# An adding transfer, two rounds for the two largest logits, larger vector instructions and a new order in a gated mix of a long convolution and a routed block

## The chip, the cores and the metric

The kernel runs on one core of a Trainium2 chip. Its engines are TensorE (PE; its weight loads are listed as PEld), VectorE (DVE), ScalarE (ACT), GpSimd (POOL) and SyncE (SP), which here only issues transfers. The metric is the device time of one execution in microseconds; the figure used is the median of several.

## The reference

Two results of the same input `x` (2048 tokens, 512 channels, bfloat16) are mixed token by token by a sigmoid gate.

```python
x = A_u
g = sigmoid((x * gate_w).sum(-1, keepdims=True))
# a: a state-space convolution: per channel a kernel K of 2048 lags, applied by FFT
dt = exp(log_dt)[:, None];  A = A_re + 1j * A_im;  dB = dt * (B_re + 1j * B_im)
P = exp((dt * A)[:, :, None] * l)              # 512 x 128 modes x 2048 lags
K = einsum("dn,dnl,dn->dl", C, P, dB).real
y = irfft(rfft(x, 4096) * rfft(K, 4096))[:2048] + x * Dskip
# b: two tokens are routed through a gated block
r = x @ w_r;  idx = argsort(-r)[:2]
b = x;  b[idx] += ((silu(x[idx] @ w_gate) * (x[idx] @ w_up)) @ w_down) * sigmoid(r[idx])
out = g * y + (1 - g) * b
```

## The kernel before

The kernel is one list of 558 operations, made by the function's helpers in the order of the source. Two hand-kept lists decide how it runs: `PLAN` gives every operation its place in one global order and, by its second number, which of its possible engines runs it; `BANKS` gives the PSUM banks. Each engine, and SP and POOL as issuers of transfers, runs its operations in PLAN's order, strictly one after the other; `emit_plan` adds the semaphore waits that the data need. So an operation that waits holds everything behind it on its engine.

The convolution is done in two blocks of 1024 tokens with a transform of 1024 points that leaves even and odd parts apart, and the modes are summed through a factorisation of each lag into a coarse and a fine part. The channels are worked in two halves (hf or c, 0 and 1). The stages, in the names of the program:

- *Set-up*: the parameters are loaded (`nat0` to `nat5`) and turned on PE by the identity matrix `CI` (`turned`, L572), which is loaded as `cia` (L525). `al` is the first DVE operation, the decay rates; ACT then runs exponentials of it (`ep`, `eq`, `ek`), and the phases follow on DVE (`bs`, `bn`, `hi`, `lo`, `psi` and others, part polar). `kw` holds the modes' weights, and its polar form goes over `ln`, `ab`, `lr`, `rec` on ACT and `sm`, `qx`, `pz`, `as` on DVE.
- *transform(m)* for block m: the loads of u (`ul`, L549) and of the transform's constants (`fl`, L551), each in two parities, are multiplied on PE (L870), evicted with factor 1 or -2 (`fwe`, `fwo`), and summed: `vb` are two transfers from POOL that add one buffer to another in SBUF (L881, L883), `v1` and `v0` two DVE sums of 2048 elements, `w1` and `w0` four DVE sums of 1024 elements per block (L886 to L888).
- *moduli, weigh*: products of the exponentials on DVE.
- *coarse(hf), fine(hf)*: PE adds up phases in PSUM (L681, L686), ACT takes sines (L437); coarse multiplies them into the table TP on DVE (`ns`, `pi`, `pr`), fine into TQ by the weighting `qm` (L727), five instructions of 2048 elements per half.
- *rows*: the transposed input `xt` is loaded by a transposing transfer (L565), PE makes the gate's and the router's logits (`log`, L744), DVE copies them. The two largest logits and their token numbers are found in four rounds of `gmax` (L766): a reduction of 16 to 1 per partition, a matmul with the identity that brings all 128 partitions' values to each partition, and a reduction of 128 to 1 from PSUM; twice for the value, twice for the index, with `cand`, `sel` and `mask` between them. Small sigmoids run on POOL. The two rows of u are gathered (`gu`), turned (`gat`), copied by ACT (`xs`), and go through the weights `wg`, `wu`, `wd`. `uc` (L839) copies u to a table in HBM, into which `sc` writes the two changed rows; `ue` and `u2` load from it. `z1` is ACT's scaling of the result by `rs`, which comes from POOL (`rsf`).
- *lags(c)*: PE sums the modes (`kmm`, L923), the result is evicted (`kae`), re-ordered by selecting matmuls (`sel`, L937) and evicted (`kce`, `kcx`); *spectrum(c)* (L962, L967) needs the constants `kn` in four pieces (L1143) and is evicted as `khe`, `khf`.
- *products(c,j)* on DVE (L1007, and sums such as `acc`, `yr`, `yi`, `pq`, `b0`, `b2`, `b13`), partly summed on PE (`ac`, L1030 to L1034); *inverse(c,j)* on PE (L1109 to L1114), evicted with the gate as scale (`ive`, L1125, L1129) and sent out. `residual` makes the diagonals `rd` that add the gated input on PE.

Most DVE operations are recorded at the line of their helper: `TT` is L408, so groups under L408 mix many stages.

Of the kernel before, what the change touches and what calls it, by code (L numbers as in the profile page):

```python
# [9 lines left out]
BF = mybir.dt.bfloat16  # L10
# [169 lines left out]
PLAN = [(0, 0), (4, 0), (5, 0), (6, 0), (7, 0), (8, 0), (9, 0), (10, 0), (11, 0), (12, 0), (13, 0), (14, 0), (3, 0), (27, 0), (1, 1), (48, 0),  # L180
# [47 lines left out]
NG = 4  # L228
# [91 lines left out]
def bass_gated_mix__ssm_conv_s4__moe_arch_mod__prompt_kernel(nc, A_u, A_A_re, A_A_im, A_B_re, A_B_im, A_C_re, A_C_im, A_log_dt, A_Dskip,  # L320
# [15 lines left out]
    for m_ in range(2):  # L336
        for q_ in range(2):
            for r_ in range(4):
                cf[:, 128 + (m_ * 2 + q_) * 4 + r_] = 4096.0 - token(m_, q_, r_)
    cf[0, 144] = 1.0  # L340
    cf[1, 145] = 1.0
    cf[0, 147] = -1.0
    cf[1, 148] = -1.0
    cf[:, 149] = 1.0e-36
    cf[:, 150] = alt
    cf[:, 151] = -alt
    cf_c = nc.inline_tensor(cf, "c_f32").ap()
    near, far = lag_mats()
# [892 lines left out]
```

## Time and profile before

| | |
|---|---|
| median of 3 runs | 147.81 us (147.77 to 147.84) |
| the profiled execution's own time | 148.18 us |
| its span, first to last instruction | 146.4 us |
| granted TensorE clock | 0.987 |
| PE busy | 128.3 us (88%), 1302 instructions |
| DVE busy | 135.5 us (93%), 174 instructions |
| ACT busy | 114.5 us (78%), 162 instructions |
| POOL busy | 18.1 us (12%), 30 instructions |
| moved by DMA | 26.46 MB, mean 181 GB/s |
| chain that ended last | DVE 44%, PE 33%, ACT 18%, issue 3% |

Busy times count instructions from start to end. Matmuls and vector instructions overlap their neighbours a little, so busy shares of a row can pass what is really used; the distance between two starts is the surer measure. The chain that ended last goes back from the last instruction, at each step to what released it or to the instruction before it on its engine. A group in the list by line and form gives busy time, mean nanoseconds of one instruction, and the idle time ahead of it. A transfer's row gives the KB of one and the time from issue to landing.

### The profile page before, as it was taken

What the parts mean: (1) busy time and instruction counts of PE and PEld (TensorE: products, weight loads), DVE (VectorE), ACT (ScalarE), POOL (GpSimd) and SP (SyncE); (2) the same over time, 40 slices, a digit from 0 to 9 for tenths busy, and PEclk for the clock granted to TensorE, in tenths of its full rate; (3) what the DMA queues carried; (4) which work ended last, traced back from release to release, by engine and by line L of the source; (5) the groups of instructions that cost most, each with busy time, mean ns of one, the idle gap of its engine ahead of it and who ended that gap; (6) DMA issues with size and microseconds to landing.
All of it is one profiled execution on the core that took longest, in us unless ns stands there. A gap on an engine that the chain in (4) does not pass through costs nothing.

```text
span 146.4 us, 3151 instructions
## 1 busy us (share of the span) xinstructions
PE 128.3 (88%) x1302; PEld 89.0 (61%) x1309; DVE 135.5 (93%) x174; ACT 114.5 (78%) x162; POOL 18.1 (12%) x30
## 2 busy tenths in 40 slices
PE   7956719999999979999979998888999898999992
PEld 3842306654434656566735886865888676778881
DVE  0699999989999999999999999999999999999962
ACT  3699999799999989699957878998499734517731
POOL 2000000180304804145310000000000000000000
PEclk9999999689999999999999999999999999999999
DMA  4779999899970809989646693735380050001345
GB/s 135 248 242 236 278 271 258 317 356 321 297 169 0 143 6 318 468 311 285 129 145 177 148 425 158 203 72 222 21 288 0 0 146 4 0 0 40 107 138 150
DMA packets 23741, 26.46 MB, mean 181 GB/s; under 512 B 9224, under 2 KB 20112, under 8 KB 23568
## 3 DMA queue, kind: packets, MB, share of 16 engines
q1 hardware_dynamic: 21134, 23.46, 52.4%
q0 software_dynamic: 1088, 2.10, 7.9%
q10 hardware_dynamic: 1506, 0.72, 1.7%
q8 instruction: 10, 0.16, 0.5%
q14 instruction: 3, 0.02, 0.0%
HBM read 19.85 MB, written 4.20 MB: 164 GB/s over the span
## 4 chain that ended last, share of the span: by engine, by line
DVE 44%; PE 33%; ACT 18%; issue 3%; POOL 0%; DVEq 0%; POOLq 0%
DVE RB L408 36%; ACT RB L437 11%; PE psm L1114 10%; ACT RB L428 6%; PE psm L962 5%; PE psm L1030 4%; DVE RB L434 3%; PE psm L1109 2%; PE psm L937 2%; PE psm L1034 2%; PE psm L1032 2%; DVE RB L706 2%; PE psm L535 2%; PE psm L681 1%; ACT L1186 1%
## 5 line engine op out<-in xcount | busy, mean ns | idle before, releaser
L408 DVE TENSOR_TENSOR RB<-RB 128x2048 bf16<-128x2048 bf16 (+8 forms) x120 | 113.0, 987 | 1.4 <-ACT RB L437 0.2
L428 ACT ACTIVATE RB<-psm 128x1024 bf16<-128x1024 f32 (+7 forms) x44 | 38.1, 898 | 15.4 <-PE psm L1034 9.2
L437 ACT ACTIVATE RB<-psm 128x1024 bf16<-128x1024 int16 (+1 forms) x37 | 36.5, 1033 | 6.4 <-PE psm L686 2.8
L1114 PE MATMUL psm<-RB 128*128 128x256 bf16 x160 | 22.3, 273 | 0.0
L681 PE MATMUL psm<-RB 128*128 128x256 f16 (+1 forms) x112 | 21.1, 336 | 0.2 <-ACT RB L428 0.2
L870 PE MATMUL psm<-RB 128*128 128x512 bf16 x61 | 15.0, 383 | 5.8 <-ACT RB L428 3.8
L437 ACT ACTIVATE RB<-RB 128x512 bf16<-128x512 f32 (+5 forms) x32 | 16.7, 591 | 1.3 <-DVE RB L408 1.2
L1114 PEld LDWEIGHTS psm<-RB 128*128 128x128 bf16 x160 | 15.7, 98 | 1.8
L686 PE MATMUL psm<-RB 128*128 128x512 f16 x44 | 13.5, 393 | 2.8 <-ACT RB L437 2.8
L962 PE MATMUL psm<-RB 128*128 128x256 bf16 x128 | 15.1, 273 | 0.8 <-ACT RB L428 0.8
L681 PEld LDWEIGHTS psm<-RB 128*128 128x128 f16 x112 | 10.8, 101 | 8.0 <-issue 0.5
L870 PEld LDWEIGHTS psm<-RB 128*128 128x128 bf16 x64 | 6.0, 100 | 14.5 <-ACT RB L428 4.7
L962 PEld LDWEIGHTS psm<-RB 128*128 128x128 bf16 x128 | 12.3, 98 | 3.4 <-ACT RB L428 1.6
L1125 ACT ACTIVATE RB<-psm,RB 128x256 bf16<-128x256 f32 x25 | 10.2, 472 | 5.2 <-PE psm L1114 4.2
L923 PE MATMUL psm<-RB 128*128 128x80 bf16 x256 | 10.4, 198 | 0.5 <-ACT RB L428 0.4
L923 PEld LDWEIGHTS psm<-RB 128*128 128x128 bf16 x256 | 9.7, 96 | 1.7 <-ACT RB L428 1.0
L1109 PE MATMUL psm<-RB 128*128 128x256 bf16 x32 | 8.7, 273 | 0.6 <-DVE RB L408 0.4
L428 ACT ACTIVATE RB<-psm,RB 128x1024 bf16<-128x1024 f32 (+1 forms) x9 | 9.2, 1062 | 0.0
L686 PEld LDWEIGHTS psm<-RB 128*128 128x128 f16 x44 | 3.5, 100 | 6.7 <-ACT RB L437 5.9
L1030 PE MATMUL psm<-RB 128*128 128x512 bf16 x21 | 6.5, 380 | 0.8 <-ACT RB L428 0.6
L883 POOL DMA_DIRECT2D RB<-RB x2 | 2.6, 1321 | 32.6 <-ACT RB L428 32.6
L434 DVE CAST RB<-psm 128x1024 bf16<-128x1024 f32 (+3 forms) x6 | 6.4, 1062 | 0.0
(71 smaller groups left out, 119.7 us busy)
## 6 DMA issues: line engine op xcount, KB each, us to landing
RB<-in_A_u_dram SPq DMA_DIRECT2D x8, 256.0 KB, 4.4
RB<-RB POOLq DMA_DIRECT2D x4, 512.0 KB, 9.8
RB<-c_near SPq DMA_DIRECT2D x4, 512.0 KB, 6.5
RB<-c_inv SPq DMA_DIRECT2D x1, 2048.0 KB, 10.4
RB<-u_routed SPq DMA_DIRECT2D x2, 1024.0 KB, 5.4
RB<-in_B_w_gate_dram SPq DMA_DIRECT2D x1, 1792.0 KB, 9.4
RB<-in_B_w_up_dram SPq DMA_DIRECT2D x1, 1792.0 KB, 16.8
RB<-in_B_w_down_dram SPq DMA_DIRECT2D x1, 1792.0 KB, 7.5
```

The source lines that it names most:

```text
L408: return P.add(name, [(eng, c_dve(n, mode) if eng == DVE else 1.0, lambda h: h.tensor_tensor(out=o(), in0=a_(), in1=b_(), op=op))], rd, wr ...
L428: return lambda h: h.activation(out=o(), in_=a_(), func=ACTF.Copy, scale=scale() if callable(scale) else scale)
L434: return P.add(name, [(ACT, c_act(n), f_act(o, a_)), (DVE, c_dve(n, 1), lambda h: h.tensor_copy(o(), a_()))], rd, wr, **kw)
L437: return P.add(name, [(ACT, cost or c_act(n), lambda h: h.activation(out=o(), in_=a_(), func=func, scale=scale))], rd, wr, table=table, **kw)
L681: r = h.matmul(P32(t, 0, 0, 128, 256 * l0, (1, 256 * nl)), DGM(0, 128, (DD.index(d) + 2) * 128, (1, 128)), src(0, 128, col + hf * CW, (0, ...
L686: r = h.matmul(P32(t, b, 0, 128, 0, (1, 512)), DGM(0, 128, 0, (1, 128)), DGM(0, 128, 128 + c_, (0, 512)), start=False, stop=False, skip_gr ...
L870: x = h.matmul(P32(t, b, 0, 128, 0, (1, 512)), FM(0, 128, 2048 * par + 1024 * pl + 512 * i + 256 * q + 128 * b, (1, 128)), U(0, 128, ((m * ...
L923: x = h.matmul(P32(t, q // 6, 0, 128, (q % 6) * 80, (1, 80)), TPv(0, 128, ri * 16384 + c * 8192 + r * 128, (1, 128)), TQv(0, 128, c * 1024 ...
L962: x = h.matmul(P32(t, kt // 2, 0, 128, (kt % 2) * 256, (1, 256)), KN(0, 128, 2048 * KNP[2 * pl + hc] + 512 * g + 128 * kt, (1, 128)), KC[c ...
L1030: r = h.matmul(P32(t, kt, 0, 128, 0, (1, 512)), CI(0, 128, 0, (1, 128)), f(k, 0, 512), start=(k == 0 and hc == 1), stop=False, skip_group_ ...
L1109: h.matmul(o, RD(0, 128, (tb + 8) % 16 * 128, (1, 128)), UE[q](0, 128, r * 256, (1, 256)) if early else U2(0, 128, tb * D + c * CW, (1, 25 ...
L1114: x = h.matmul(o, G(0, 128, (pl * 4 + kt) * 1024 + (r * 2 + q) * 128, (1, 128)), PQ(0, 128, r * 1024 + kt * 256 + pl * 256 if quarter else ...
```

## The change

The new list has 546 operations. By edit:

- In block 1 the sum `v0` leaves DVE; a third adding transfer from POOL (`vd`) does it, after `v1`.
- `w1` and `w0` become one DVE sum of 2048 elements each per block. So that both planes have the same sign, one plane of the odd part is built from the other parity's summand first (the order of r in `transform`).
- `qm`, the weighting, takes groups 0 and 1, then 2 and 3, then 4: two instructions of 4096 elements and one of 2048 per half.
- The two largest logits: `top` replaces `gmax`, with DVE's eight-largest instruction (`max`). Two rounds instead of four; each brings the largest and second of every partition to all partitions by two matmuls, and takes the eight largest of 256 in PSUM. The two token numbers are found in one round, by coding the rank into the candidates. Two small POOL operations (`ix1`, `ix2`) are added ahead of `idx`.
- The identity `cia` is built on POOL, by a memset and two affine selects, instead of being loaded.
- The constants of the transform and `kn` lie in HBM piece by piece, so that each load is one contiguous block.
- `hh` moves from POOL to DVE.
- `PLAN` and `BANKS` are new. DVE has 163 operations instead of 174, ACT 143 instead of 147 (its transfers included), POOL 31 instead of 26, PE 161 instead of 163 groups of matmuls. Among others, `xt` is issued ahead of the transform's second-parity loads, `uc` ahead of `wg` and `gu`, `c_inv` (the inverse's constants) ahead of the last two pieces of `kn`, and some evictions change sides between ACT and DVE.

```diff
-        DMA("cia", lambda h: [h.dma_start(CI(0, 128, 0, (1, 256)), dr(id_c, 0, (640, 128), (1, 256)))], [], [bCIA], 64, rate=200.0, also=(ACT,))
+        P.add("one", [(POOL, 0.25, lambda h: h.memset(ONE(0, 128, 0, (1, 128)), 1.0))], [], [bONE])
+        P.add("id0", [(POOL, 0.25, lambda h: h.memset(CI(0, 128, 0, (1, 256)), 0.0))], [], [bCIA])
+        P.add("id1", [(POOL, 0.35, lambda h: h.affine_select(out=CI(0, 128, 0, (1, 128)), in_=CI(0, 128, 0, (1, 128)), compare_op=ALU.not_equal, fill=1.0, base=0, pattern=[[-1, 128]], channel_multiplier=1))], [bCIA], [bCIA])
+        P.add("id2", [(POOL, 0.35, lambda h: h.affine_select(out=CI(0, 128, 128, (1, 128)), in_=CI(0, 128, 128, (1, 128)), compare_op=ALU.not_equal, fill=-1.0, base=0, pattern=[[-1, 128]], channel_multiplier=1))], [bCIA], [bCIA])
...
-                TT("qm", q, q, lambda G_=G_: MQ(0, 128, hf * 5120 + G_ * 1024, (0, 2), (1, 1024)), ALU.mult, bQS[G_][hf] + [bMW[hf] if G_ < 2 else bMF[G_][hf]], [bQF[G_][hf]], 2048)
+                for gs in ((0, 1), (2, 3), (4,)):
+                    if gs[-1] != G_:
+                        continue
+                    q = lambda gs=gs: TQv(0, 128, hf * 10240 + gs[0] * 1024, (5120, 2), (1, 1024 * len(gs)))
+                    TT("qm", q, q, lambda gs=gs: MQ(0, 128, hf * 5120 + gs[0] * 1024, (0, 2), (1, 1024 * len(gs))), ALU.mult, ..., 2048 * len(gs))
...
+        def top(src, bsrc, tag):
+            P.add("gm", [(DVE, 0.17, lambda h: h.max(out=RT["pm"](0, 128, 0, (1, 8)), in_=src(0, 128, 0, (1, 16))))], [bsrc], [bRT["pm"]])
+            t = P.pst(1, "gm")
+            def gt(h, t=t):
+                for k in range(2):
+                    r = h.matmul(P32(t, 0, 0, 128, 128 * k, (1, 128)), RT["pm"](0, 128, k, (0, 128)), CF(0, 128, 0, (1, 128)), start=True, stop=True)
+                return r
+            MM("gt", gt, [bRT["pm"], bCF], [t], 1.0)
+            P.add("gm2", [(DVE, 0.43, lambda h, t=t: h.max(out=RT[tag](0, 128, 0, (1, 8)), in_=P32(t, 0, 0, 128, 0, (1, 256))))], [t], [bRT[tag]])
...
+        top(rb2, brb2, "m1")
+        STT("cand", row(cand, 0, 16), row(rb2, 0, 16), one1("m1"), idx, ALU.is_ge, ALU.add, [brb2, bRT["m1"], bCF], [bcand], 16)
+        STT("cand", row(cand, 0, 16), row(rb2, 0, 16), two1("m1"), row(cand, 0, 16), ALU.is_ge, ALU.mult, [brb2, bRT["m1"], bcand], [bcand], 16)
+        top(cand, bcand, "v1")
...
-            TT("v0", vs(0, 0, 0, 1024), vs(0, 0, 0, 1024), vs(1, 1, 0, 1024), ALU.add, bVs[m][0][0] + bVs[m][1][1], bVs[m][0][0], 2048)
-            for hc in (1, 0):
-                for pl in range(2):
-                    TT("w%d" % hc, vs(1, hc, pl, 512), vs(1, 0, pl, 512), xs(1 - pl, 512), ALU.add if pl == hc else ALU.subtract, [bVs[m][1][0][pl], bXO[m][1 - pl]], [bVs[m][1][hc][pl]], 1024)
+            if m in [1]:
+                DMA("vd", lambda h, lo=lo: [h.dma_start(lo(0, 0), lo(1, 1), accum_op=ALU.add)], bVs[m][0][0] + bVs[m][1][1], bVs[m][0][0], 512, eng=POOL, issue=1.3, lat=3.8, rate=155.0)
+            else:
+                TT("v0", vs(0, 0, 0, 1024), vs(0, 0, 0, 1024), vs(1, 1, 0, 1024), ALU.add, ..., 2048)
+            ws = lambda hc: (lambda: V(0, 128, vo[m][1] + hc * 1024, (vo[m][3] - vo[m][1], 2), (512, 2), (1, 512)))
+            xw = lambda: XO[m](0, 128, 1024 * m + 512, (-1024 if m else 1024, 2), (-512, 2), (1, 512))
+            TT("w1", ws(1), ws(0), xw, ALU.subtract, bVs[m][1][0] + bXO[m], bVs[m][1][1], 2048)
...
+                TT("w0", ws(0), ws(0), xw, ALU.add, bVs[m][1][0] + bXO[m], bVs[m][1][0], 2048)
...
-            DMA("kn", lambda h, i=i: [h.dma_start(KN(0, 128, 2048 * KNP[i], (1, 2048)), dr(kn_c, 2048 * i, (8192, 128), (1, 2048)))], [], [bKN[i]], 512, rate=330.0)
+            DMA("kn", lambda h, i=i: [h.dma_start(KN(0, 128, 2048 * KNP[i], (1, 2048)), dr(kn_c, 2048 * 128 * i, (2048, 128), (1, 2048)))], [], [bKN[i]], 512, rate=370.0)
```

More of the change, by code (lines that the diff above doesn't have):

```diff
@@ L407, in TT @@
         def TT(name, o, a_, b_, op, rd, wr, n, mode=2, eng=DVE, **kw):
-            return P.add(name, [(eng, c_dve(n, mode) if eng == DVE else 1.0, lambda h: h.tensor_tensor(out=o(), in0=a_(), in1=b_(), op=op))], rd, wr, **kw)
+            return P.add(name, [(eng, c_dve(n, mode) if eng == DVE else 1.8, lambda h: h.tensor_tensor(out=o(), in0=a_(), in1=b_(), op=op))], rd, wr, **kw)
         def TS(name, o, a_, s1, op0, rd, wr, n, mode=1, s2=None, op1=None, eng=DVE, **kw):
@@ L414, in TS @@
                 f = lambda h: h.tensor_scalar(out=o(), in0=a_(), scalar1=s1() if callable(s1) else s1, scalar2=s2() if callable(s2) else s2, op0=op0, op1=op1)
-            return P.add(name, [(eng, c_dve(n, mode) if eng == DVE else 1.0, f)], rd, wr, **kw)
+            return P.add(name, [(eng, c_dve(n, mode) if eng == DVE else 1.8, f)], rd, wr, **kw)
         def TSA(name, o, a_, s1, s2, rd, wr, n, mode):
@@ L421, in PC @@
         def PC(name, o, a_, rd, wr):
-            return P.add(name, [(POOL, 0.9, lambda h: h.tensor_copy(o(), a_()))], rd, wr)
+            return P.add(name, [(POOL, 1.8, lambda h: h.tensor_copy(o(), a_()))], rd, wr)
         def STT(name, o, a_, sc, b_, op0, op1, rd, wr, n, **kw):
@@ L470, in bass_gated_mix__ssm_conv_s4__moe_arch_mod__prompt_kernel @@
         RT = {}; bRT = {}
-        for k in ("pm", "m1", "v1", "m2", "v2", "rs0", "rsr", "rs", "ix0", "ix1"):
-            RT[k], bRT[k] = small("rt_" + k, 4, F32)
+        for k, n_ in (("pm", 8), ("m1", 8), ("v1", 8), ("rs0", 1), ("rsr", 1), ("rs", 1), ("ix0", 1), ("ix1", 1)):
+            RT[k], bRT[k] = small("rt_" + k, 4 * n_, F32)
         IDX, bIDX = small("idx", 4, I32)
@@ L531, in bass_gated_mix__ssm_conv_s4__moe_arch_mod__prompt_kernel @@
         row = lambda v, c=0, n=D: (lambda: v(0, 128, c, (1, n)))
-        P.add("one", [(POOL, 0.3, lambda h: h.memset(ONE(0, 128, 0, (1, 128)), 1.0))], [], [bONE])
         twm = P.pst(1, "hm")
@@ L768, in gmax @@
             t = P.pst(1, "gm")
-            MM("gt", lambda h, t=t: h.matmul(P32(t, 0, 0, 128, 0, (1, 128)), RT["pm"](0, 128, 0, (0, 128)), CF(0, 128, 0, (1, 128)), start=True, stop=True), [bRT["pm"], bCF], [t], 0.5)
-            P.add("gm2", [(DVE, 0.29, lambda h, t=t: h.tensor_reduce(out=RT[tag](0, 128, 0, (1, 1)), in_=P32(t, 0, 0, 128, 0, (1, 128)), axis=AX.X, op=ALU.max))], [t], [bRT[tag]])
+            def gt(h, t=t):
+                for k in range(2):
+                    r = h.matmul(P32(t, 0, 0, 128, 128 * k, (1, 128)), RT["pm"](0, 128, k, (0, 128)), CF(0, 128, 0, (1, 128)), start=True, stop=True)
+                return r
@@ L788, in token_of @@
+        TS("ix1", one1("ix1"), two1("v1"), 1.0, ALU.is_ge, [bRT["v1"], bCF], [bRT["ix1"]], 1, s2=lambda: CF(0, 128, 153, (1, 1)), op1=ALU.mult, eng=POOL)
+        TT("ix2", one1("ix0"), one1("ix0"), one1("ix1"), ALU.add, [bRT["ix0"], bRT["ix1"]], [bRT["ix0"]], 1, 1, eng=POOL)
+        STT("idx", lambda: IDX(0, 2, 0, (1, 1)), lambda: CF(0, 2, 148, (1, 1)), lambda: RT["v1"](0, 2, 1, (1, 1)), lambda: RT["ix0"](0, 2, 0, (1, 1)), ALU.mult, ALU.add, [bRT["v1"], bRT["ix0"], bCF], [bIDX], 1)
         def token_of(h, k):
@@ L863, in transform @@
                 tiles = [P.pst(2, "fw") for pl in range(2)]
-                for i, r in enumerate((par + 2, par)):
+                for i in range(2):
                     for pl in range(2):
+                        r = par + 2 * (i == 0) if not (par and not pl) else par + 2 * i
                         def fw(h, t=tiles[pl], i=i, r=r, pl=pl, par=par):
```

55 lines of the change are left out of this document (27 added, 28 removed), and 68 rows, old and new, of the table PLAN.

## The prediction

> **What bounds the kernel now.** I read the page first (busy shares), then the busy time by stretch, then the chain that ended last, then the groups by form, and last the queues.
>
> ```profile
> span 146.4 us, 3151 instructions
> ...
> PE 128.3 (88%) x1302; PEld 89.0 (61%) x1309; DVE 135.5 (93%) x174; ACT 114.5 (78%) x162; POOL 18.1 (12%) x30
> ```
>
> ```profile
> 4.90:30.00 25.10, 17.51 (x144) 10.70 (x145) 24.42 (x40) 23.40 (x38) 1.30 (x3) 0.93 1.00 271
> 30.00:60.00 30.00, 28.21 (x249) 15.68 (x250) 29.14 (x44) 28.30 (x34) 10.55 (x15) 1.00 0.74 204
> 60.00:90.00 30.00, 27.92 (x362) 19.30 (x360) 29.90 (x35) 24.51 (x30) 5.39 (x9) 1.00 0.78 255
> 90.00:140.00 50.00, 47.26 (x507) 37.94 (x509) 49.38 (x54) 35.10 (x57) 0.00 (x0) 1.00 0.29 82
> ```
>
> The columns after the length are PE, PEld, DVE and ACT busy. From 4.9 to 140 us DVE is busy 132.8 of 135.1 us: it is the bound for the whole body, and a DVE instruction taken out there is time taken out, as long as something else does not become late. ACT is nearly full until 60 us (51.7 of 55.1) and free after that; PE is nearly full from 90 us on. From 140 us on there is only a tail of a few matmuls, four evictions and the output.
>
> ```profile
> 43.83 1.24 DVE RB L408
> 45.09 4.51 DVE RB L408 x4
> ...
> 96.91 0.27 PE psm L1109
> ```
>
> In the chain, four independent products start 1.13 us apart (4.51 over 4), but one whose successor needs its result keeps the next waiting 1.26 (43.83 to 45.09): a gap of about 0.12. From 96.91 on the chain runs over PE, though DVE is just as full there: both matter.
>
> **The change part by part.** Durations are of this profiled execution, whose own time is 148.18 us for a span of 146.4; the median of the runs is 147.81, 0.37 lower, so I take the sum off 147.81.
>
> ```profile
> L408 DVE TENSOR_TENSOR RB<-RB 128x2048 bf16<-128x2048 bf16 x60 | 71.3, 1218 | 0.7
> L408 DVE TENSOR_TENSOR RB<-RB 128x1024 bf16<-128x1024 bf16 x31 | 20.5, 686 | 0.2
> L408 DVE TENSOR_TENSOR RB<-RB 128x4096 bf16<-128x4096 bf16 x4 | 9.1, 2281 | 0.0
> L770 DVE TENSOR_REDUCE RB<-psm 128x1 f32<-128x128 f32 x4 | 1.1, 284 | 0.4 <-PE psm L769 0.4
> L767 DVE TENSOR_REDUCE RB<-RB 128x1 f32<-128x16 f32 x4 | 0.7, 168 | 0.1
> L425 DVE SCALAR_TENSOR_TENSOR RB<-RB 128x16 f32<-128x16 f32 x2 | 0.4, 210 | 0.0
> L414 DVE TENSOR_SCALAR RB<-RB 128x16 f32<-128x16 f32 x1 | 0.2, 234 | 0.0
> L408 DVE TENSOR_TENSOR RB<-RB 128x16 f32<-128x16 f32 x1 | 0.2, 175 | 0.0
> L759 DVE RECIPROCAL RB<-RB 128x16 f32<-128x16 bf16 x1 | 0.2, 246 | 0.0
> L759 DVE RECIPROCAL RB<-RB 128x1 f32<-128x1 bf16 x1 | 0.2, 157 | 0.0
> ```
>
> An instruction starts some 0.083 before the one ahead of it ends (1.218 against the spacing of 1.13), so I count 1.135, 0.603 and 2.20 us for 2048, 1024 and 4096 elements.
>
> *Adding transfer*: one sum of 2048 less: -1.13.
>
> *Larger sums*: eight of 1024 become four of 2048: 8 x 0.603 - 4 x 1.135 = -0.28. *Larger weighting*: ten of 2048 become four of 4096 and two of 2048: 11.35 - 11.07 = -0.28.
>
> *Largest two*: twelve instructions go, 4 x 0.284 + 4 x 0.168 + 2 x 0.210 + 0.234 + 0.175 = 2.64 busy; the 0.4 wait for the broadcast matmul and the gaps of this dependent chain about cancel the overlap, so 2.64 of the line. Six come: two reductions of 16 (0.085 of spacing), two of 256 from PSUM, two 0.21 with gaps of 0.12. Eight-largest has no row. Lower end: as a reduction, 0.284 + 128 x 0.00104 = 0.42, spacing 0.33 (0.00104 us an element is 0.284 less 0.15 over 128). Upper end: the reciprocal's rate, (0.246 - 0.157) / 15 = 0.006 an element, 1.67 us for 256. I take the lower, since the reduction is the same walk over the same PSUM row: 0.17 + 0.66 + 0.5 = 1.33, so -1.3; the other end is 2.7 dearer.
>
> ```profile
> L434 DVE CAST RB<-psm 128x1024 bf16<-128x1024 f32 x2 | 2.4, 1212 | 0.0
> L434 DVE CAST RB<-psm 128x960 bf16<-128x960 f32 x2 | 2.3, 1151 | 0.0
> L1159 DVE TENSOR_TENSOR RB<-RB 128x1024 bf16<-128x1024 bf16 x1 | 1.2, 1206 | 0.0
> ```
>
> *Sides in the new order* (PLAN's second number picks the engine): off DVE go one spectrum eviction (1.13) and the residual's diagonals (1.12); onto it come one lag eviction of 960 (1.07), and one of 320, a negation, a 32x256 copy and three tiny ones (hh among them), by their sizes an estimated 1.2: nothing on balance (+0.05). On ACT the diagonals are eight instructions, about 2.8 us, laid beside the selecting matmuls, where ACT is free after 60 us: nothing, or up to 1 us if the spectrum's evictions come late by it.
>
> *Gaps*: counted in the two lists, outside the largest-two chain, some 29 neighbours need the result just ahead, 18 in the new one: 11 x 0.12 = -1.3.
>
> ```profile
> 4.91 0.69 DVE L408 TENSOR_TENSOR RB<-RB,psm 128x512 f32<-128x512 bf16 x1 [4.91 <-PE psm L572]
> ...
> 1.31 0.38 ACTq L525 DMA_DIRECT2D RB<-c_id  x1
> 3.87 0.60 ACT L437 ACTIVATE RB<-psm 128x512 bf16<-128x512 f32 x1 [1.86 <-PE psm L539]
> ...
> RB<-c_id ACTq DMA_DIRECT2D x1, 64.0 KB, 2.3
> ...
> 0.72 0.20 POOL L532 MEMSET RB<- 128x128 bf16 x1 [0.29 <-POOLq L1226]
> ```
>
> *Identity on POOL*: the identity lands at 1.31 + 2.3 = 3.6 now, the turns (L572) start at 3.8, DVE at 4.91, while the other operand is ready at 4.47. A memset of 256 and two affine selects after 0.92 cost 0.2 each at the memset's rate, 1.2 at the dearer small POOL row below: ready at 1.5 to 4.0. The first turn alone then frees DVE at 4.55: -0.35, between -0.35 and +0.2.
>
> *Constants by piece* have no row for the contiguous form; their loads are two or more us ahead of use, so nothing either way; cover gone, PE waits for 512 KB, 1.9 us at the 271 GB/s of the first stretch.
>
> ```profile
> 8.71 11.56 SPq L446 DMA_TRANSPOSE RB<-in_A_u_dram  x1
> ...
> RB<-in_A_u_dram SPq DMA_TRANSPOSE x1, 13.7
> ...
> DMA packets 7932, 2.07 MB, mean 259 GB/s; under 512 B 7911, under 2 KB 7925, under 8 KB 7932
> ...
> L744 PE MATMUL psm<-RB x64: 167/172/173, 24.2 to 26.2; 128*128 128x2 bf16 x64
> ```
>
> *The new order's head*: the logits' copy moves from DVE 27.9 to about 20.4 (sum of the DVE rows ahead of it). It needs the transposed load plus 2.3 us of matmuls. Now issued at 8.7 and landed at 22.4, its 256 B packets move from 14 to 22 us (the third row is of that window), behind two loads of 512 KB. The new list puts it ahead of those, at about 6.4; then its packets can run from about 9.5, and 7.5 us of them end at 17 to 18: no wait. If it keeps its 13.7, it lands at 20.1, the copy at 22.5: a wait of 2.0. The two loads behind it (transform 0's second half) land at 21 to 25 against a need at 24 to 26.
>
> *Waits that stay or come*: the old list carries about 1.3 us of them on DVE beside the 0.4 above. In the new one I find, adding rows on both sides: qx waits for the reciprocal on ACT (17.0 us of ACT rows after 5.25) 0.8; the second product waits for c_near's last piece, which now lies behind the 2 MB of c_inv on SP, 0.9; the first lag eviction and the first product 0.5; spectrum 1's evictions are due within 0.6 us of the product that reads them. With something unseen, 2.8, between 1 and 6.
>
> ```profile
> L883 POOL DMA_DIRECT2D RB<-RB x2: 1266/1321/1376, 28.7 to 64.3; - x2
> ...
> DMA to landing us min/median/max: 5.1/9.8/14.5
> ...
> L412 POOL TENSOR_SCALAR RB<-RB 128x16 bf16<-128x16 bf16 x1 | 1.2, 1172 | 0.1
> ...
> L414 POOL TENSOR_SCALAR RB<-RB 128x16 bf16<-128x16 bf16 x1 | 0.2, 208 | 0.0
> ```
>
> *Queues*: the new transfer waits for v1 (DVE, about 67.5) and holds POOL 1.3 us; even 14.5 us later its sum is there at 82, and its first reader is a product at about 104. Behind it on POOL stand sgo twice, omg and rsf, 0.2 to 1.2 each; ACT's z1 at about 75.5 needs rsf, ready at 72 to 74.7: covered by 1 to 3 us. If not, z1 holds ACT and the spectrum's evictions. Small POOL rows of one shape differ sixfold here (0.208, 1.172). The Trainium skill, SBUF — State Buffer, section Who interferes with whom, says that a VectorE instruction with two SBUF inputs blocks a GpSimd one that reads SBUF until it ends; by that rule the 4096-element weighting beside omg and rsf makes them later by about 1 us, which the cover still holds; the spread of the rows agrees with it. ix1 and ix2 come before idx with 6 us of DVE work between: covered.
>
> *Tail*: same last matmuls and outputs, 0, within 0.6.
>
> **Sum**: -1.13 - 0.28 - 0.28 - 1.3 + 0.05 - 1.3 - 0.35 = -4.6; old waits -1.3, new ones +2.8: -3.1. 147.8 - 3.1 = 144.7.
>
> **The rivals.**
>
> *PE sets the end.* Its last stretch starts when spectrum 1 is done, which follows fine 1's last weighting; by the same sum DVE reaches that 2.6 us earlier (the gaps saved behind it, some 0.5, left out). One more inverse piece (0.55) comes after spectrum 1, and PE's late waits may add 0.5: -1.5, 146.3. Against it: lag evictions start on a free ACT in the new list.
>
> *Eight-largest is dear*: -3.1 + 2.7: 147.4.
>
> *The transposed load keeps its length*: -3.1 + 2.0 = 146.7.
>
> *The larger instructions do not run at two elements a cycle* (the change not doing what it says): the four sums with reversed blocks at 1 ns an element, 4 x 1.05 = +4.2: 148.9. The b13 sums already have reversed blocks among the 686 ns group: unlikely.
>
> *Slower: the two chosen rows arrive late.*
>
> ```profile
> RB<-in_A_u_dram SPq DMA_DIRECT2D x1, 256.0 KB, 10.0
> ...
> 40.41 0.20 DVE L425 SCALAR_TENSOR_TENSOR RB<-RB 2x1 int32<-2x1 f32 x1
> ...
> 47.55 0.17 ACT L428 ACTIVATE RB<-psm 128x8 bf16<-128x8 f32 x1
> ...
> RB<-in_B_w_gate_dram SPq DMA_DIRECT2D x1, 1792.0 KB, 9.4
> ...
> u_routed<-in_A_u_dram SPq DMA_DIRECT2D x1, 12.6
> ```
>
> A 256 KB load issued behind the gate weights took 10.0 us: SP's loads go in turn. The new list puts the 2 MB copy of u and the gate weights ahead of the two gathered rows, whose turned form ACT copies (xs, now at 47.55) at about 40.9, in line with the sines. Now xs starts 7.1 after idx (40.41), with ACT busy ahead of it; the new list has idx at 34, so xs at 41.1 or sooner, no wait worth naming if the queue is empty by 38. From 17.5 on it carries 1.9 MB of smaller loads, the copy's 2 MB and 1.8 MB of gate weights: at the 271 GB/s of the first stretch above, 21 us, so 38.5. At the rows' full times (24 + 12.6 + 9.4) it empties at 46: ACT waits 6, DVE, which runs a us behind the sines, 4.5: +1.4, 149.2. It decides from a landing after about 44. The Trainium skill, DMA: Bandwidth & Descriptors, section Queues, rings and completion order, says that each engine takes a ring's descriptors in order; by that the gathered rows wait for all of both, which the 10.0 agrees with.
>
> **How the numbers follow.** Forecast, 142.8 to 146.0: 0.58. PE's end and the long transposed load, 146.0 to 147.4: 0.20; dear eight-largest, about 147.4, and no change: 0.09, of which 0.07 within 0.2%; slower (late rows, slow sums, unseen): 0.10; better than 142.8: 0.03. 0.2%, 0.3 us, is what these runs can tell from no change. Faster 0.83, same 0.07, slower 0.10. Range for 8 in 10: 142.8 (new waits about 1 us: -5.0) to 147.8 (new waits 6, or no change).
>
> **What would show it.** Right: DVE busy about 131 (one eviction of 512 leaves its tail too), first DVE at 4.5, spacing 2.2 in the weighting, transposed load landed by 18, last b13 sum ended near 137 instead of 140. Wrong: a wait ahead of xs on ACT, of the logits' copy or of the second product on DVE over 2 us, eight-largest over 1 us, or DVE ending early and PE still running on.

## The result, and the profile after

The changed kernel takes 147.21 us in the median of 20 runs, the kernel before 148.26 beside it on the same chip: ratio 0.991 (95% interval 0.989 to 0.994), some 1.3 us faster. The forecast was 3.1 us faster, 144.7. The profiled execution takes 147.33 us against 148.18: 0.85 less. Its page:

```profile
span 145.5 us, 3147 instructions
...
PE 128.9 (89%) x1303; PEld 88.9 (61%) x1309; DVE 131.8 (91%) x163; ACT 115.4 (79%) x167; POOL 27.3 (19%) x35
```

DVE is busy 3.7 us less, about as forecast (131.8, "about 131"), but the span is only 0.9 us shorter: DVE now stands still more. Groups by form:

```profile
L411 DVE TENSOR_TENSOR RB<-RB 128x2048 bf16<-128x2048 bf16 x55 | 65.7, 1219 | 0.5
...
L411 DVE TENSOR_TENSOR RB<-RB 128x4096 bf16<-128x4096 bf16 x8 | 18.2, 2287 | 1.0 <-ACT RB L431 0.9
...
L898 POOL DMA_DIRECT2D RB<-RB x1 | 1.2, 1200 | 6.4 <-DVE RB L411 6.4
...
L782 DVE MAX8 RB<-psm 128x8 f32<-128x256 f32 x2 | 0.9, 428 | 1.0 <-PE psm L779 1.0
...
L775 DVE MAX8 RB<-RB 128x8 f32<-128x16 f32 x2 | 0.4, 178 | 0.1
```

Eight-largest cost the lower end of its bounds (0.18 and 0.43 us), and the larger instructions keep the pace of the others: 2.29 us for 4096 elements, 1.22 to 1.23 for each of the four sums with reversed blocks, as for every other sum of 2048. What DVE waited for (total us, times, longest):

```profile
DVE RB L411 <- PE psm L577: 4.9, 1, 4.9
DVE RB L1150 <- PE psm L1135: 2.1, 3, 1.6
DVE RB L782 <- PE psm L779: 1.0, 1, 1.0
DVE RB L411 <- ACT RB L431: 0.9, 2, 0.6
DVE RB L428 <- POOL RB L411: 0.8, 1, 0.8
DVE RB L411 <- DMA RB<-in_A_C_im_dram: 0.5, 1, 0.5
```

The first row is the start, the second the tail. The other four are the new waits: before the first eight-largest of 256 (its broadcast matmul), before the first two products (evictions of spectrum 0), before `idx` (POOL), and before the second `bc` (the load of C's imaginary part). A shorter one, 0.23, stands before the logits' copy. Counted as the distance of two starts less an undisturbed spacing, which takes in the restart, all these are 3.9 us up to the last b13 sum, against 1.55 before. "Waits" below are counted so.

The tail is 6.27 us after the end of the last b13 sum (140.12 before, 139.27 after), in both kernels and within 0.02 in every run below: that end is the time. The profiled execution of idx_later below is one of its slow ones (its ratio is not), so it is read up to 45 us only.

### The profile page after: what moved, and what is told of

It is laid out like the page before. It is cut to its first block, busy times and chain, and to the rows that moved or that the text cites. A ratio compares the mean times of both kernels' runs of the same rounds, so it can differ in the third digit from the quotient of the medians.

```text
span 145.5 us, 3147 instructions
## 1 busy us (share of the span) xinstructions
PE 128.9 (89%) x1303; PEld 88.9 (61%) x1309; DVE 131.8 (91%) x163; ACT 115.4 (79%) x167; POOL 27.3 (19%) x35
## 4 chain that ended last, share of the span: by engine, by line
DVE 61%; PE 15%; ACT 8%; DMA 6%; POOL 5%; issue 2%; SPq 1%; ACTq 0%
DVE RB L411 54%; ACT RB L440 6%; POOL RB L417 5%; DMA RB<-c_near 3%; DMA RB<-in_A_C_im_dram 3%; ACT RB L431 3%; PE psm L686 2%; PE psm L1135 2%; PE psm L882 2%; DVE RB L437 2%; PE psm L691 2%; PE psm L752 1%; PE psm L983 1%; PE psm L944 1%; SPq L533 1%
## 5 line engine op out<-in xcount | busy, mean ns | idle before, releaser
L411 DVE TENSOR_TENSOR RB<-RB 128x2048 bf16<-128x2048 bf16 (+9 forms) x111 | 110.4, 1045 | 2.0 <-ACT RB L431 0.9
L431 ACT ACTIVATE RB<-psm 128x1024 bf16<-128x1024 f32 (+7 forms) x42 | 37.5, 918 | 12.6 <-PE psm L1055 8.8
L440 ACT ACTIVATE RB<-psm 128x1024 bf16<-128x1024 int16 (+1 forms) x37 | 36.2, 1015 | 6.3 <-PE psm L691 2.8
L882 PE MATMUL psm<-RB 128*128 128x512 bf16 x60 | 16.8, 408 | 3.4 <-DVE RB L434 2.8
L1146 ACT ACTIVATE RB<-psm,RB 128x256 bf16<-128x256 f32 x27 | 10.7, 491 | 4.9 <-PE psm L1135 4.3
L417 POOL TENSOR_SCALAR RB<-RB 128x1 f32<-128x1 f32 (+3 forms) x6 | 11.8, 1973 | 4.0 <-DVE RB L782 3.8
L411 POOL TENSOR_TENSOR RB<-RB 128x1 f32<-128x1 f32 (+3 forms) x5 | 1.5, 304 | 38.9 <-DVE RB L782 22.4
L1051 PE MATMUL psm<-RB 128*128 128x512 bf16 x22 | 6.7, 380 | 0.2
```

Of the source, the lines that this page charges most:

```text
L411: return P.add(name, [(eng, c_dve(n, mode) if eng == DVE else 1.8, lambda h: h.tensor_tensor(out=o(), in0=a_(), in1=b_(), op=op))], rd, wr ...
L417: f = lambda h: h.tensor_scalar(out=o(), in0=a_(), scalar1=s1() if callable(s1) else s1, scalar2=s2() if callable(s2) else s2, op0=op0, op ...
L431: return lambda h: h.activation(out=o(), in_=a_(), func=ACTF.Copy, scale=scale() if callable(scale) else scale)
L440: return P.add(name, [(ACT, cost or c_act(n), lambda h: h.activation(out=o(), in_=a_(), func=func, scale=scale))], rd, wr, table=table, **kw)
L882: x = h.matmul(P32(t, b, 0, 128, 0, (1, 512)), FM(0, 128, 2048 * par + 1024 * pl + 512 * (r < 2) + 256 * q + 128 * b, (1, 128)), U(0, 128, ...
L1146: x = h.activation(out=OT[k](0, 128, ocol(q, r), (1, 256)), in_=P32(t, 0, 0, 128, q * 256, (1, 256)), func=ACTF.Copy, scale=SGF["gc"](0, 1 ...
```

## The experiments

All are the changed kernel with the edit shown, and each ratio is to the kernel before, timed beside it. `PLAN`'s entries are named instead of numbered. The runs were made in groups, and the ratio of one program moves between them: the changed kernel itself has 0.989 in the group of idx_later, index_on_dve and broadcast_first (after_again) and 0.994 in that of best_eviction (after_last; 0.989 to 0.992 was expected). The other groups have no run of it. For each run the trace gives the start of `idx`, the end of the last b13 sum, and the waits up to it:

| run | ratio (95%) | waits | idx | b13 end | between |
|---|---|---|---|---|---|
| changed kernel | 0.991 (0.989-0.994) | 3.9 | 36.20 | 139.27 | 103.1 |
| after_again | 0.989 (0.983-0.994) | 4.0 | 36.37 | 139.34 | 103.0 |
| after_last | 0.994 (0.991-0.997) | 2.9 | 35.47 | 138.52 | 103.1 |
| idx_later | 0.998 (0.993-1.004) | | 37.58 | | |
| index_on_dve | 0.984 (0.979-0.990) | 2.9 | 36.02 | 139.04 | 103.0 |
| broadcast_first | 0.982 (0.976-0.988) | 2.4 | 34.69 | 137.88 | 103.2 |
| broadcast_again | 0.984 (0.980-0.988) | 1.7 | 34.70 | 137.46 | 102.8 |
| both_head | 0.989 (0.985-0.993) | 3.0 | 35.82 | 139.20 | 103.4 |
| head_order | 0.992 (0.989-0.996) | 2.3 | 35.90 | 138.66 | 102.8 |
| narrow | 0.991 (0.988-0.995) | 1.9 | 35.31 | 138.27 | 103.0 |
| sum_back | 0.998 (0.994-1.002) | 3.4 | 35.73 | 139.93 | 104.2 |
| sums_early | 0.988 (0.984-0.993) | 4.3 | 36.40 | 139.53 | 103.1 |
| all_order | 0.989 (0.985-0.993) | 2.9 | 35.67 | 139.07 | 103.4 |
| inverse_later | 1.011 (1.006-1.016) | 5.1 | 35.07 | 140.54 | 105.5 |
| gaps_fewer | 0.997 (0.994-1.000) | 5.0 | 35.84 | 139.77 | 103.9 |
| gaps_out | 1.019 (1.013-1.025) | 9.2 | 36.16 | 143.70 | 107.5 |
| waits_out | 1.003 (0.999-1.008) | 4.5 | 35.37 | 140.50 | 105.1 |
| best_eviction | 0.987 (0.981-0.993) | 2.8 | 34.44 | 138.25 | 103.8 |

best_order (1.014, 1.008-1.020) stands with inverse_later below. Two things to read: from `idx` on, the changed kernel and the versions near it all need 102.8 to 103.4 us; and the same program reaches `idx` at 35.5 to 36.4.

**What idx waits for.** after_again is the base of its group.

> The changed kernel itself, as the base of this group. Both theories: 0.991 of the kernel before, DVE's waits for other engines again near 3.9 us up to the last b13 sum (0.60 before bc, 1.05 before the eight-largest of 256, 0.90 before idx, 0.65 and 0.45 before the first two products).

idx_later puts `idx` behind the next product:

```diff
-... cm, idx, wg, fw, pi, ns ...
+... cm, wg, fw, pi, idx, ns ...
```

> Only idx, the VectorE step that waits for GpSimd's ix0, ix1 and ix2, stands one product (pi, 1.14 us) later in VectorE's order. Theory A (GpSimd's ix0 takes its 6.3 us by itself): GpSimd is done at 36.2 whatever VectorE does, idx starts at 36.5 without a wait, and the kernel is 0.9 us faster than the changed one (0.985 of before). Theory B (ix0 can't get at SBUF while VectorE's instructions follow one another without a gap, and ended at 35.6 only because VectorE had run out of work at 35.4): with one more product ahead ix0 lasts about 1.1 us longer, the wait before idx is 0.6 to 0.9 again, and the time is that of the changed kernel within 0.3 us.

POOL and DVE in the timeline (start, us; in brackets the idle time before it), the changed kernel first:

```profile
29.29 6.61 POOL L417 TENSOR_SCALAR RB<-RB 128x1 f32<-128x1 f32 x2 [3.76 <-DVE RB L782]
```

```profile
33.16 2.22 DVE L411 TENSOR_TENSOR RB<-RB 128x2048 bf16<-128x2048 bf16 x2
36.20 0.21 DVE L428 SCALAR_TENSOR_TENSOR RB<-RB 2x1 int32<-2x1 f32 x1 [0.82 <-POOL RB L411]
```

and idx_later:

```profile
29.53 7.74 POOL L417 TENSOR_SCALAR RB<-RB 128x1 f32<-128x1 f32 x2 [3.77 <-DVE RB L782]
```

```profile
33.40 3.35 DVE L411 TENSOR_TENSOR RB<-RB 128x2048 bf16<-128x2048 bf16 x3
37.58 0.20 DVE L428 SCALAR_TENSOR_TENSOR RB<-RB 2x1 int32<-2x1 f32 x1 [0.82 <-POOL RB L411]
```

With one more product ahead, POOL's two one-element instructions took 1.13 us longer, and the wait came out the same (0.90 in both). So theory A is out: what DVE runs beside it holds `ix0` (6.31 of the 6.61 us here), which ended some 0.2 us after DVE had run dry. That it always takes a break of DVE, as theory B has it, is not so: see broadcast_first below. The Trainium skill, SBUF — State Buffer, section Who interferes with whom, says that a VectorE instruction with two SBUF inputs contends with a GpSimd one that reads SBUF, and that of two that contend the later waits until the other has finished. The trace agrees in kind, but the hold here was longer than one instruction: eight of DVE's ran meanwhile. Theory B's time did not come out either: the ratio is 0.7% over the changed kernel's 20 runs, 1.0% over after_again's, where it forecast 0.2% at most. Why stays open; the index comes 1.2 to 1.4 us later, and so does what is gathered by it.

index_on_dve removes `eng=POOL` from `ix0`, `ix1` and `ix2`:

> ix0, ix1 and ix2 run on VectorE instead of GpSimd, at the same places of the order. Both theories of ix0: the 0.90 us wait before idx goes, three instructions of one element come, some 0.1 to 0.2 us each with their gaps: 0.3 to 0.6 us faster than the changed kernel. msb on GpSimd, which now comes first there, lasts until VectorE leaves a gap (theory B: over 2 us; theory A: under 0.5 us). Rival for the whole: ScalarE's sines are the bound up to 60 us, and what VectorE saves here it waits for later: no difference at the end.

The wait before `idx` is gone. The ratio, 0.984 beside after_again's 0.989, points the way that was forecast, but their intervals overlap, and in the one profile the last b13 sum ends only 0.3 us earlier than in after_again's. `msb` now took 0.35 us on POOL, at 24.7, beside DVE's dependent chain of candidates, where the same instruction had taken 3.0 at 36.2. A wait of 0.98 before the second eight-largest had come instead.

**What is paid in the head.**

```diff
-... log, pa (coarse 0), ..., qx, gt, ...
+... log, ..., qx, gt, pa (coarse 0), ...
```

> On TensorE the first broadcast of the two largest (fp32 matmuls) stands ahead of the first phases of coarse 0 instead of behind them. Theory (a wait on VectorE is paid in full, since VectorE is full behind it): the 1.05 us wait before the eight-largest of 256 goes and the end comes 0.8 to 1.05 us earlier than in the changed kernel (0.984 to 0.986 of before). Rival (ScalarE's sines are the bound here, since the first one of coarse 0 starts as much later): a wait of VectorE for a sine takes its place between 27 and 50 us, and the time is that of the changed kernel within 0.3 us.

> broadcast_first once more, as the base of this group: the span about 144.1, VectorE's waits 2.4 us up to the last b13 sum, 0.982 of before. Rival (its 1.2 us against the changed kernel were the chip of that group): 0.99 of before.

`idx` starts 1.5 us earlier than in the first profile of the changed kernel, and the end comes 1.4 to 1.8 us earlier (0.6 to 1.1 against its fastest profile, after_last). The waits of broadcast_first:

```profile
DVE RB L411 <- ACT RB L431: 1.1, 2, 0.6
DVE RB L411 <- DMA RB<-in_A_C_im_dram: 0.8, 1, 0.8
DVE RB L434 <- PE psm L752: 0.2, 1, 0.2
```

Neither broadcast nor `idx` is among them, though `ix0` is still on POOL. POOL, then DVE:

```profile
28.68 3.66 POOL L417 TENSOR_SCALAR RB<-RB 128x1 f32<-128x1 f32 x2 [3.91 <-DVE RB L782]
```

```profile
32.55 2.22 DVE L411 TENSOR_TENSOR RB<-RB 128x2048 bf16<-128x2048 bf16 x2
34.69 0.20 DVE L428 SCALAR_TENSOR_TENSOR RB<-RB 2x1 int32<-2x1 f32 x1
```

DVE ran the same instructions from the second eight-largest to `idx`, again without a break, and `ix0` took 1.73 us and not 6.31. It did so in all four profiles with this order on TensorE and the index on POOL (sums_early and best_eviction below are the others); in the nine with the old order it took 6.31 (7.44 in idx_later). In the four, DVE had waited 0.13 to 1.26 us just before that eight-largest; in the nine it had not. Whether this is what lets POOL through was not tested. So what the edit took away in every profile is the 0.90 before `idx`, which its theory did not name. The wait that it did name, before the first eight-largest, was 1.05 in one profile of the old order, 0.23 to 0.62 in six and absent in two.

This is the fastest version found: its two intervals end at 0.9875, where that of the changed kernel's 20 runs begins at 0.9885. Against after_again (0.983 to 0.994) they overlap, and from index_on_dve it is not told apart. Two more steps on it brought nothing:

```diff
 head_order: broadcast_first, ix0, ix1, ix2 on DVE, and
-... bs, bc, bn, bc ...
+... bs, bn, bc, bc ...
 both_head: broadcast_first, ix0, ix1, ix2 on DVE, and
-... fw, fw, gt (second), pa ...
+... fw, gt (second), fw, pa ...
```

> Of the kernel with the waits out only its first part, up to 40 us: the first broadcast ahead of coarse 0's first phases on TensorE, ix0, ix1 and ix2 on VectorE, bn ahead of the product that waits for C's imaginary part. Theory (a wait of VectorE is paid in full where nothing else is moved with it): 0.4 to 1.05 (broadcast) + 0.4 (index, 0.90 less three tiny instructions) + 0.34 (bn) = 1.2 to 1.8 us faster than the changed kernel, about 0.98 of before. Rival (ScalarE's sines are the bound from 40 us on): VectorE waits there instead, under 0.5 us faster.

> broadcast_first with the second broadcast, too, ahead of the transform's matmuls on TensorE, and with ix0, ix1 and ix2 on VectorE. Theory: no wait before either eight-largest and none before idx; against broadcast_first only three tiny instructions (0.45 us) come, so 0.2 to 0.5 us slower than that one. Rival (GpSimd held msb and with it the tanh on ScalarE, so the sines after 38 us were late): up to 0.7 us faster than broadcast_first.

In head_order one wait of 0.84 for the second broadcast and one of 0.60 for the transform's matmuls took the place; in both_head, beside the waits that stayed, one of 0.55 for the transform's matmuls. TensorE in the first 30 us differs from run to run of one program, and with it what is late. Windows of the changed kernel (length, PE, PEld, DVE, ACT and POOL busy, granted clock, DMA share, GB/s), then of sums_early:

```profile
10.00:20.00 10.00, 7.29 (x59) 3.19 (x61) 9.90 (x14) 10.00 (x18) 0.00 (x0) 0.83 1.20 251
20.00:30.00 10.00, 9.48 (x70) 5.74 (x70) 8.72 (x21) 9.97 (x14) 1.27 (x2) 0.83 1.03 388
```

```profile
10.00:20.00 10.00, 6.97 (x32) 2.42 (x34) 9.94 (x14) 10.00 (x18) 0.00 (x0) 0.75 1.17 242
20.00:30.00 10.00, 8.87 (x85) 6.09 (x85) 7.88 (x20) 8.13 (x11) 0.55 (x1) 0.57 1.04 385
```

At 0.57 sums_early waited 0.81 for the logits and 1.26 for the second broadcast, though up to 70 us it is the same program as broadcast_again, which had 1.00 and 0.83, no wait for the logits and 0.15 for that broadcast. after_again, the changed kernel itself, had 0.66 and 1.00 and no wait before the first eight-largest. What sets the clock in this stretch was not tried.

**Which work is paid.**

```diff
 sum_back
-            if m in [1]:
+            if m in []:
 narrow: each qm of 4096 as two of 2048, each w1 and w0 as two of 1024
```

> The adding transfer of block 1 is undone: the sum runs on VectorE again, at the same place of the order (between pi and pr of coarse 1). Theory (VectorE is full there, so an instruction on it is paid in full): one instruction of 2048 more, 1.13 us, less one gap of 0.12 that it breaks, so the last b13 sum ends 1.0 us later than in the changed kernel, and the kernel takes 1.0 us more. Rival (the slot was idle or the transfer costs as much elsewhere): within 0.3 us of the changed kernel.

> The larger weighting and sums are undone in size alone: each weighting of 4096 elements is two of 2048, each sum of 2048 is two of 1024, in place, one behind the other. Theory: eight more instructions, each some 0.07 us (2 x 1.135 - 2.20 and 2 x 0.603 - 1.135): 0.56 us more than the changed kernel. Rival (reversed blocks or the longer instruction run slower than two elements a cycle): no difference, or faster.

(In narrow the sums' second plane gets the signs of the kernel before, so `w1` and `w0` are exchanged there and the output is not the reference's; every one of those sums took 0.68 to 0.69 us, as the others of 1024.) sum_back needs some 1.1 us more behind `idx` (104.2 against 102.8 to 103.4): in this order the adding transfer's gain is real and whole. narrow has 0.7 us more DVE busy time (132.5 against 131.8) and needs no more behind `idx`. The two stretches before the products, the changed kernel first:

```profile
83.50 4.50 DVE L411 TENSOR_TENSOR RB<-RB 128x4096 bf16<-128x4096 bf16 x2 [0.56 <-ACT RB L431]
...
90.07 2.29 DVE L411 TENSOR_TENSOR RB<-RB 128x4096 bf16<-128x4096 bf16 x1 [0.37 <-ACT RB L431]
```

```profile
82.73 2.29 DVE L411 TENSOR_TENSOR RB<-RB 128x4096 bf16<-128x4096 bf16 x1 [0.29 <-ACT RB L431]
...
88.72 3.75 DVE L411 TENSOR_TENSOR RB<-RB 128x256 bf16<-128x256 bf16 x3
```

(The last row's group of three holds the second product, without a wait.) The waits before both products shrink from 1.10 to 0.37, by about what the narrow instructions take longer, and the first product starts 47.4 us after `idx` instead of 47.3: there the end is set by the evictions of spectrum 0, not by DVE.

**The second product and the order behind 70 us.**

```diff
 inverse_later
-... gload (c_inv), u8, ..., kn, kn, kt ...
+... u8, ..., kn, kn, gload (c_inv), kt ...
 sums_early: broadcast_first, and
-... v0, qm (fine 1), kce, w1, w0, w1, w0 ...
+... v0, w1, kce, w0, w1, w0, qm (fine 1) ...
```

> SyncE issues the 2 MB of c_inv behind c_near's last two pieces instead of ahead of them, nothing else. Theory of the forecast (c_near's last piece waits behind c_inv): it lands about 2 us after its issue instead of 4.4, the fourth spectrum product no longer waits for it, and the 0.45 us wait before the second product on VectorE goes: 0.4 us faster. Rival (its issue, which has to wait for the last sum that reads the place, is what makes it late, and ScalarE's chain behind it is as long): under 0.2 us.

> broadcast_first with the first weighting of fine 1 behind the four sums instead of ahead of them (the first sum still waits for the adding transfer until about 75). Theory: the last sum ends 1.5 us earlier, c_near's last piece is issued and lands as much earlier, and the 0.45 to 0.6 us wait before the second product goes: 0.3 to 0.6 us faster than broadcast_first. Rival (the first product's wait, which ScalarE's evictions set, is the longer one and grows by what is saved): within 0.2 us of broadcast_first.

Transfers between 70 and 95 us, the same row in the changed kernel and in inverse_later, and behind it a wait of DVE in inverse_later:

```profile
RB<-c_near SPq DMA_DIRECT2D x2, 512.0 KB, 3.8
```

```profile
DVE RB L411 <- DMA RB<-RB: 2.8, 1, 2.8
```

c_near's pieces land 3.8 us after issue with c_inv ahead or behind. They are issued at 80.1 and 82.5, as the last two sums that read their place end: that makes them late. But the small transfers `kt`, now behind 2 MB, took 7.2 us and more instead of 3.6 and held `ku` 2.8 us. best_order carried the same edit, and the same wait at 4.0.

sums_early took the product's waits away and got one of 1.23 before `w1` instead, as long as the two of broadcast_first that it removed:

```profile
69.81 1.20 POOL L898 DMA_DIRECT2D RB<-RB  x1 [6.40 <-DVE RB L411]
```

```profile
75.91 1.22 DVE L411 TENSOR_TENSOR RB<-RB 128x2048 bf16<-128x2048 bf16 x1 [1.15 <-DMA RB<-RB]
```

L898 is `vd`, the adding transfer of this change. `w1` writes over the plane that `vd` reads, and so cannot start before it has landed, at 75.88. The sum that left DVE now bounds how early the four sums can come; in the changed kernel's order `vd` lands at 75.8 and `w1` starts at 77.6. all_order adds it to both_head and the `bn` exchange, and waited 1.52 at that place. waits_out is an earlier such bundle (1.12 there), with a spectrum product ahead of a phase on TensorE, and on ACT a sine behind two evictions; fine 1 then waited 1.00 and 0.91.

> The changed kernel's instructions with another order: the first broadcast ahead of coarse 0's first phases on TensorE; ix0, ix1 and ix2 on VectorE; the sums of the second half ahead of fine 1's first weighting (so c_near's last pieces can be loaded some 2 us earlier); spectrum 0's second product ahead of a phase on TensorE; bn ahead of the product that waits for C's imaginary part. Theory (VectorE's new waits, 3.9 us, are what the forecast missed, and they are paid in full): the waits fall to 0.5 to 1.2 us, three tiny instructions come (0.45), the last b13 sum ends near 137.0 instead of 139.2, and the kernel is 2.0 to 2.7 us faster than the changed one (about 0.975 of before). Rival (ScalarE up to 60 us or TensorE behind 90 us is the bound, VectorE's waits are slack): other waits take their place, under 1 us faster.

> both_head and sums_early together, and bn ahead of the product that waits for C's imaginary part. Theory (waits can be regained by order): 0.5 to 1.0 us faster than broadcast_first, 0.976 of before, waits under 1.5 us up to the last b13 sum. Rival (behind 60 us the end is set by the chain over TensorE and ScalarE, spectrum 0 and its evictions, so that VectorE only reaches the first product earlier and waits there): the waits before the first two products grow to 1.5 us or more, no faster than broadcast_first.

> head_order and inverse_later together, and three of the exchanges of gaps_fewer (lo behind kw, a reciprocal and z0 between dependent neighbours). Theory, as a sum: 1.2 to 1.8 + 0.4 + 0.35 = 2.0 to 2.5 us faster than the changed kernel, 0.974 of before. Rival (a wait moved is a wait that turns up elsewhere): no faster than head_order.

**The gaps.**

```diff
 gaps_out
-... lo, kw, sq ... sgr, ns, pi ... cm, ns, ffe, pi, pr ... z0, qm, ns, pi ... w1, w0, w1, w0 ... k0c (lags 1) on DVE
+... kw, lo, sq ... ns, sgr, pi ... ns, cm, pi, ffe, pr ... qm, ns, z0, pi ... w1, w1, w0, w0 ... k0c (lags 1) on ACT
 gaps_fewer: the same with "cm, ns, ffe, pi, pr" left as it was
```

> The changed kernel with seven pairs of dependent neighbours on VectorE taken apart by exchanging neighbours, and lags 1's copy of k0, which starts at partition 96, given to ScalarE. Theory (each dependent neighbour costs 0.117 us on a full VectorE, and the copy 0.25 with a gap of 0.114 on one more neighbour): 7 x 0.117 + 0.37 = 1.2 us faster than the changed kernel, with the gaps listed at those places gone. Rival (a gap only hides a wait that comes anyway): under 0.4 us.

> The kernel with the gaps out, without two of its exchanges: the moduli's product stays ahead of coarse 1's negation, and the eviction of the gate product (ffe) stays ahead of coarse 1's first product. Theory: it was the ffe, 2 us later, for which TensorE waited 2.2 us at 50 us (its bank), and the sines behind it; the remaining exchanges bring 5 x 0.117 + 0.37 = 0.95 us against the changed kernel. Rival (VectorE's gaps are not what sets the time, or ScalarE's extra copy or the sums' order cost as much): no difference to the changed kernel, within 0.3 us.

gaps_out has 21 gaps of 0.1 us or more instead of 28, and is the slowest of all. TensorE at 52 us, and DVE just ahead:

```profile
52.24 1.89 PE L882 MATMUL psm<-RB 128*128 128x512 bf16 x4 [2.24 <-DVE RB L434]
```

```profile
52.00 0.18 DVE L434 CAST RB<-psm 128x28 bf16<-128x28 f32 x1
```

The eviction `ffe`, 0.18 us, had come 2 us later, behind one product and a wait, and TensorE stood for its bank; 2.17 us of DVE's waits for a sine followed. In gaps_fewer that wait is gone, so it was this pair of exchanges; but the other five gaps and the copy, 0.95 us by their sum, brought nothing either, and gaps_fewer needs 0.8 us more behind `idx` than the changed kernel: the waits before the two products grew from 1.10 to 1.95 (my reading is the copy on ACT and the order of the sums; the two were not taken apart).

**Behind 90 us.**

> The changed kernel on the chip of this group: 0.989 to 0.992 of before, as in its other groups.

best_eviction is broadcast_first with lags 1's eviction of 320 on ACT (its number in `PLAN` 0 instead of 1).

> broadcast_first with lags 1's eviction of 320 (0.40 us at 94.7) on ScalarE instead of VectorE. Theory (behind 90 us VectorE has no waits up to the last b13 sum, so that its work there is paid in full): the last b13 sum 0.4 us earlier than in broadcast_first, 0.979 of before, 1.5 us under the changed kernel. Rival (TensorE's selection of lags 1 waits for ScalarE's evictions, 1.3 us at 95, and comes 0.4 later): the time of broadcast_first, 0.982 to 0.984, or up to 0.4 us more.

No gain: 0.987 stands beside 0.994 of the changed kernel in its group, as broadcast_first's 0.982 beside 0.989. A wait of 0.36 came before a product at 105.3, and the second product waited 0.87. So 0.4 us taken out of a full stretch of DVE was not paid either.

## Why the prediction was wrong in size, step by step

Start-to-start sums up to the last b13 sum, profile against profile; the sides are what is left over:

| term | forecast | measured |
|---|---|---|
| adding transfer | -1.13 | -1.13, in full (sum_back 1.1) |
| larger sums, larger weighting | -0.56 | -0.57 of DVE's work; 0 of the time (narrow) |
| largest two, with its old wait | -1.3 | -1.32 (0.82 and 0.50) |
| sides | +0.05 | -0.19 |
| gaps | -1.3 | -0.46 |
| start | -0.35 | 0 |
| old waits, new waits | -1.3, +2.8 | -1.05, +3.87 |
| sum | -3.1 | -0.85 |

The table is of one profile of each kernel. In the changed kernel's other two the new waits are 4.0 and 2.9 us, and the last b13 sum ends at 139.34 and 138.52. So the forecast's 2.8 for the new waits was met once and missed by over 1 us twice, while the gaps, the start and the wait before `idx` (0.90) came out nearly the same in all three: these steps failed whatever the execution.

*New waits*, mis-sized by 1.1 in this profile. The three named came near in size (2.2 forecast, 2.15 found) by luck, not in cause. "qx waits for the reciprocal" (0.8): `qx` started in time, and the eight-largest behind it waited 1.05 for its broadcast, which stood behind coarse 0's phases on TensorE, an order that the forecast did not follow. The second product and the first (0.9 and 0.5): 0.45 and 0.65, and c_inv ahead of c_near changes nothing. Unseen were C's imaginary part (0.60, where DVE had had `bn` to do before) and `idx` (0.90), a step that the forecast called "covered": it priced POOL's `ix1` and `ix2` by POOL's own rows against "6 us of DVE work between", when that unbroken DVE work was itself what held POOL in this list. The cited rule stood in the forecast, for `omg` and `rsf`, and was not applied to the chain that DVE waits for.

*Gaps*, mis-sized by 0.8: outside the largest-two chain 29 neighbours were forecast before and 18 after; the traces have 30 and 26, of 0.114 to 0.118 us each but one. The count took data needs alone. A copy that starts at partition 96 (`k0e`, `k0c`) has a gap of 0.114 on both sides though its neighbours share no data with it, and the new order has two `k0c` on DVE, so that six of the 26 are such. The first `k0c` in the timeline, where unhindered instructions overlap by 0.083:

```profile
53.05 2.36 DVE L411 TENSOR_TENSOR RB<-RB 128x2048 bf16<-128x2048 bf16 x2
55.44 0.22 DVE L963 COPY RB<-RB 32x256 bf16<-32x256 bf16 x1
55.70 1.22 DVE L411 TENSOR_TENSOR RB<-RB 128x2048 bf16<-128x2048 bf16 x1
```

The Trainium skill, VectorE: DVE Perf Modes, section Two Vector instructions with no wait between them, gives as a model that an instruction whose operand starts in another group of 32 partitions than the one before is held until that one has finished; the rows agree.

*Start*: the step "the identity lands at 3.6, the turns start at 3.8" took a near time for a cause. The timeline of the changed kernel:

```profile
1.85 0.29 POOL L531 TENSOR_SCALAR_AFFINE_SELECT RB<-RB 128x128 bf16<-128x128 bf16 x1
...
3.23 0.60 PE L544 MATMUL psm<-RB 1*128 1x512 bf16 x1
...
3.77 1.53 PE L577 MATMUL psm<-RB 128*128 128x128 bf16 x8
3.87 0.60 ACT L440 ACTIVATE RB<-psm 128x512 bf16<-128x512 f32 x1 [1.85 <-PE psm L544]
...
4.91 0.69 DVE L411 TENSOR_TENSOR RB<-RB,psm 128x512 f32<-128x512 bf16 x1 [4.91 <-PE psm L577]
```

The identity is ready at 2.1, and the turns still start at 3.77, as before: they stand behind the broadcast of dt on TensorE, and the first DVE instruction stays at 4.91.

*Right*: the direction, the adding transfer, eight-largest, the sides, the logits (transposed load issued at 6.5, its row 11.8 us; a 0.23 wait), `vd`'s issue without anyone waiting, the tail. *PE sets the end* did not happen: the tail is the same 6.27 us. *The chosen rows late* did not happen in the changed kernel (`xs` at 43.98, with ACT busy ahead of it). None of the forecast's signs of being wrong came: they looked for one wait over 2 us, and the loss was six of 0.23 to 1.05.

That waits were a loss is shown in the head, where one exchange on TensorE, which also took the wait before `idx` away, ended the last b13 sum 0.6 to 1.9 us earlier than in the three profiles of the changed kernel; that all could be regained is not: behind `idx` every exchange tried was answered by a wait of its size or more.

## What to carry to other kernels

A saturated engine's waits are not a list of separate items: where three engines feed each other in turn, a removed wait or instruction counts only if what the next step needs from the others is earlier too, so ask for each term which wait ends last at the place where it is saved. Price a helper engine's small instruction on DVE's critical path by what DVE runs beside it, not by its duration elsewhere. And before an instruction is exchanged with its neighbour for a tenth of a microsecond, look for the PSUM bank or buffer that it frees.

## What the runs showed that I had not expected

- Two one-element POOL instructions lasted 6.6 us beside an unbroken run of DVE instructions, and ended with DVE's first break; in four other profiles they lasted 3.7 us beside the same unbroken run.
- TensorE's granted clock between 10 and 30 us took values from 0.57 to 1.00, and differed between executions of programs that are the same there (0.75 and 0.57 in sums_early, 1.00 and 0.83 in broadcast_again); the start of `idx` moved by 0.9 us between executions of one program.
- After a pause of 2.24 us on TensorE at 50 us the granted clock was 0.72 between 50 and 54 us in gaps_out; it was 1.00 there in the changed kernel. That the pause did it is not shown: after one of 1.89 us, ahead of 40.2, the changed kernel had 1.00.
